# Sink values from small transfers, a new order at the start, and a hold on five weight pieces

## The chip, the cores and the metric

The kernel runs on one core of a Trainium2 chip. The metric is device time in microseconds (us), the median of several executions. The engines named below are TensorE (PE, matrix products into PSUM), VectorE (DVE), ScalarE (ACT), GpSimd (POOL, which here prepares masks and issues the loads that change the type from float32 to bfloat16) and SyncE (SP, which issues plain transfers and transposing transfers).

## The reference

An attention over 4 batches, 8 heads, 768 positions and 64 features per head, in which each position sees the 128 positions up to itself and the first 4 positions (the sinks), followed by a multiplicative feed-forward part on the 3072 rows of 512 features:

```
keep = (key position < 4) | ((0 <= query - key) & (query - key < 128))
a    = softmax(q k^T / 8, over the kept keys);   x = a v   (rows: batch and position, columns: head and feature)
out  = ((x w1) * (x w2)) w3 w_out
```

Shapes: w1 and w2 are 512 x 1024, w3 is 1024 x 1024, w_out is 1024 x 512. Inputs and output are float32; the kernel multiplies in bfloat16.

## The kernel before

**Folding.** w3 w_out is computed first, on the chip, into w3o (1024 x 512), so that each row of the output needs one product with w3o instead of two. For each of eight blocks of 128 rows of w3 the block is transposed by PE (fold_w3, `tp`, 2 x 4 matmuls with the identity), copied from PSUM by DVE (L413), and multiplied with the eight blocks of w_out (fold_mm, `ph` or `pw`, 4 x 2 matmuls, two blocks sharing one `ph`). The result is copied to w3o by ACT (L445, L442). For three blocks of w3 POOL's loads change the type. The other five, and all of w_out in four pairs of blocks, come as nine uncast pieces of 512 KB, issued by SP at the very start (load_raw, L162) into buffers that are free until later: ab of both batches, and kN, qN and kqT of batch 1. ACT or DVE casts each (L418). In this text they are pieces 1 to 9 in the order of issue. `hold` makes POOL wait for the fifth piece ahead of its first load (a one-column copy to `spent`, L201).

**Attention.** Per batch, q, k and v are loaded in blocks of 128 positions (load_qkv, L108, three transfers each, in POOL's order), transposed to kqT (by PE and DVE in batches 0 and 1, by SP's transposing transfers in batches 2 and 3), and scored per pair of heads (`sc`); ACT takes the exponential, DVE multiplies with a mask (`am`), PE multiplies with v (`av`), DVE normalizes. The sinks have a product of their own: `sp` are the scores of the four sink keys of all heads, `es` their exponentials, and `vs` a matrix with the sink rows of v spread so that row 32 (h // 2) + 4 (h % 2) + s holds head h, sink s. `vs` is made by sink_values: a selection matmul of PE (`vp`, L232, with the selection matrix `pick`) and a multiply of DVE with the pattern `ones_s` (L234).

**Feed-forward.** Gates (`pg`, L391): four matmuls with w1, ACT copies, four with w2, DVE multiplies into ab. Then `po` (L452) with w3o, ACT copies, SP stores.

**What sets the order.** Every step is a task with a list of engines and estimated times. A planner (plan) goes through them three times in estimated time, choosing PE's next step by when it can start and by priority, and only the last pass emits instructions. So the tables `raws` (order of the nine pieces and the engine that casts each), `order` (POOL's loads), `nudge` (changes of single priorities), PACE (distance of score steps per batch), the arrival model landings() and the times per task decide in what order PE, ACT, DVE and SP stand. Each engine then goes through its own instructions strictly in that order and waits on semaphores. Where the planner sees PE wait over 0.5 us near the start, keep_busy emits filler matmuls (`pz`, L466) whose result is not used. PSUM has four buffers for most products and two for scores.

Of the kernel before, what the change touches and what calls it, by code (L numbers as in the profile page):

```python
# [21 lines left out]
def kernel(  # L22
# [13 lines left out]
    nc = tc.nc  # L36
# [8 lines left out]
    P = 128  # L45
# [8 lines left out]
    XPOSE = (2, 3)  # L54
# [15 lines left out]
    pick = const.tile([P, P], BF16, name="pick")  # L70
# [56 lines left out]
    def load(what, *i):  # L127
# [9 lines left out]
        else:  # L137
# [12 lines left out]
    nudge = {}  # L150
# [17 lines left out]
    casts = [load_raw(n, *x) for n, x in enumerate(raws)]  # L168
# [5 lines left out]
    nc.vector.memset(pick[:], 0.0)  # L174
    for b in range(B - 1):
        nc.vector.memset(ksbd[b][:], 0.0)

# [16 lines left out]
    pk = pick[:].rearrange("p (r x) -> p r x", x=32)  # L194
    for e in range(2):
        nc.gpsimd.tensor_copy(pk[:, :, 4 * e:4 * e + 4],
                              ident[:, 0:4].rearrange("p (r s) -> p r s", r=1).to_broadcast([P, NP, 4]))
    for b in range(B):
        nc.gpsimd.tensor_copy(vs[b][:, :, D], ones_s[:])
    if hold:  # L200
        nc.gpsimd.tensor_copy(spent[:], casts[hold - 1][1][:, 0:1])  # L201
# [27 lines left out]
    def sink_values(b):  # L229

        vp = ps_mm.tile([P, H, D], FP32, tag="mm", name="vp")
        nc.tensor.matmul(vp[:], pick[:], vN[b][:, 0, :, 0:D], start=True, stop=True)  # L232
        yield
        nc.vector.tensor_mul(vs[b][:, :, 0:D], vp[:],  # L234
                             ones_s[:].rearrange("p (h o) -> p h o", o=1).to_broadcast([P, H, D]))
        yield
# [232 lines left out]
    arrive = {}  # L469

# [10 lines left out]
    def landings(taken, RAW=2.0, POOL=3.0, DGE=1.3, RAMP=(0.6, 0.95, 0.85, 0.9)):  # L481

        queues = {"sp": [(RAW, 1.28, 1.0, [("raw",) + x[:3]]) for x in raws],
# [5 lines left out]
        while any(at[n] < len(q) for n, q in queues.items()):  # L489
# [17 lines left out]
            for n in busy:  # L507
                i = int(now - RAW) if now >= RAW else 0
                share = 1.0 if len(busy) == 1 else 0.5 if small not in "kqv" else 0.79 if n == "sp" else 0.13
                left[n][at[n]] -= 0.02 * share * (RAMP[i] if i < len(RAMP) else 1.0)  # L510
                if left[n][at[n]] <= 0.0:
                    lag, keys = queues[n][at[n]][2:]
                    for key in keys:
                        arrive[key] = now + lag
                    if n == "pool":
                        landed.append(now + lag)
                    at[n] += 1
# [12 lines left out]
    for n, ((what, i0, i1, e), ap) in enumerate(zip(raws, casts)):  # L530
        task(("c", what, i0), n, cast(e == "act", *ap), [(e, 1.04 if e == "act" else 0.69)],
             loads=[("raw", what, i0, i1)])
        made.update({(what, i): ("c", what, i0) for i in range(i0, i1)})

    def need(what, i):
        return ([made[what, i]], []) if (what, i) in made else ([], [(what, i)])

    for i in range(KFF):
        for h in range(2):
            j0, j1 = 4 * h, 4 * h + 4  # L540
            needs = [need("w3", i)]
# [20 lines left out]
    for b in range(B):  # L562
        for t in range(NT):
# [3 lines left out]
            for kb in kbs:  # L567
                if b in XPOSE:
# [8 lines left out]
            if t == 0:  # L577
                task(("sk", b), 0, sink_keys(b), [("dve", 0.2)], [("sc", b, 1, 0)])
                task(("sv", b), 2, sink_values(b), [("pe", 0.22), ("dve", 0.7)],
                     [("av", b - 2, NP - 1, NT - 1), ("av", b, 1, 0)] if b >= 2 else [], [("v", b, 0)], "mm")  # L580
            else:
# [3 lines left out]
                elif t == 1:  # L585
                    more = [(n, b, kb) for n in (("tdk", "tdq") if b in XPOSE else ("tpk",)) for kb in (4, 5)]
# [23 lines left out]
            for r in range(NP):  # L610
                after = list(qk)
                if b >= 2 and t == 0:
                    after.append(("g", b - 2, len(CHUNKS[b - 2]) - 1, KFF - 1, 1))
# [21 lines left out]
    for b in range(B):  # L635
        for c, (t0, t1) in enumerate(CHUNKS[b]):
            last_t = (t1 - 1) // 256
            us = 0.65 * (t1 - t0) / 384
            for dt in range(KFF):
                n = dt * P // 256  # L640
                pr = 1000 + 200 * b + 10 * c + dt
                war = [("p", b - 2, NB - 1)] if b >= 2 else []
                task(("g", b, c, dt, 0), pr + 0.5, gate(b, c, dt, 0), [("pe", us), ("act", 0.2 + us / 2)],
                     ([("xd", b, last_t, 0), ("xd", b, last_t, 1)] if (b, last_t) in X_XPOSE else
                      [("xt", b, NP - 2, last_t)]) + war, [("w1", n), ("w2", n)], "mm",
# [4 lines left out]
            for m in range(t0 // P, t1 // P):  # L650
                cuts = (0, DM // 2, 3 * DM // 4, DM) if (b, m) == (B - 1, NB - 1) else (0, DM)
                for n0, n1 in zip(cuts, cuts[1:]):
# [4 lines left out]
                         [("g", b, c, KFF - 1, 1), *[folded(i) for i in range(KFF)]], ring="mm")  # L657
# [6 lines left out]
    PACE = [0.0, 2.6, 5.5, 4.5]  # L664
# [4 lines left out]
    def plan(emit):  # L669
# [16 lines left out]
        def pe_pick():  # L686
            best = None
            for k in tasks.values():
# [16 lines left out]
                if k["paced"]:  # L705
                    busy = max(0.0, free["act"] - free["pe"]) + sum(q[2] for q in queue["act"])
                    est = max(est, free["pe"] + busy - BACKLOG, last_sc + (PACE[k["name"][1]]))
# [125 lines left out]
```

## Time and profile before

| what | value |
|---|---|
| median of 3 runs | 198.28 us (197.68 to 198.59) |
| profiled execution | 197.16 us, of which its span (first to last instruction) 195.5 us |
| granted TensorE clock | 1.00 of full speed |
| busy share of the span | PE 96%, DVE 59%, ACT 53%, POOL 39% |
| PE, matmuls | 187.9 us in 1818 records |

Busy time of PE holds the filler as well. "DMA share" in a view of stretches is the mean busy share of the 16 DMA engines, counted per queue, so that it can exceed 1. A row of the timeline gives start, duration, engine, line, operation, what it writes and reads, and in brackets the engine's idle time just before with what ended it. A row of the chain gives start, duration and what the work that ended last was doing then; the duration there is the time until the next step, so it shows PE's pace, while a single matmul's duration in the timeline holds its pipeline too.

### The profile page before, as it was taken

The numbers are of one execution on the slowest core, as the hardware profiler recorded it, in microseconds if no ns is written. First come the engines' busy times: TensorE is split into PE (matmuls) and PEld (weight loads), VectorE is DVE, ScalarE is ACT, GpSimd is POOL, SyncE is SP. The second block draws the span as 40 slices with busy tenths as digits, with TensorE's granted clock in tenths as the row PEclk, the third lists the DMA queues.
The fourth block names the chain that finished last, engine by engine and source line by source line (L and its number), as shares of the span: only waits on it lengthen the run. The fifth ranks groups of instructions, "written<-read, shape, count | busy, mean of one in ns | idle before, by whom it ended". The sixth has DMA issues, their size and how long they took to land.

```text
span 195.5 us, 4615 instructions
## 1 busy us (share of the span) xinstructions
PE 187.9 (96%) x1818; PEld 123.4 (63%) x1831; DVE 115.2 (59%) x276; ACT 104.2 (53%) x176; POOL 75.5 (39%) x104
## 2 busy tenths in 40 slices
PE   7689999999999999999999999999999999999993
PEld 2245566888776687888886555566666666644443
DVE  4456696755989888678575426678788344410000
ACT  4242569635776876565565646657583333333232
POOL 5189967689999953433553330000000000000000
PEclk9999999999999999999999999999999999999999
DMA  6999999999999999999999999999220200014334
GB/s 225 401 362 156 179 162 197 194 159 154 155 150 183 180 176 114 156 159 145 137 155 155 149 159 191 239 208 155 49 54 2 57 0 0 0 57 161 143 134 152
DMA packets 107429, 29.14 MB, mean 149 GB/s; under 512 B 98448, under 2 KB 102928, under 8 KB 107408
## 3 DMA queue, kind: packets, MB, share of 16 engines
q0 software_dynamic: 79520, 12.33, 90.3%
q1 hardware_dynamic: 27744, 16.46, 40.6%
q8 instruction: 14, 0.23, 0.5%
q10 hardware_dynamic: 144, 0.07, 0.1%
q14 instruction: 7, 0.06, 0.1%
HBM read 29.36 MB, written 6.29 MB: 182 GB/s over the span
## 4 chain that ended last, share of the span: by engine, by line
PE 86%; DMA 7%; POOL 3%; DVE 1%; issue 1%; SPq 1%; ACT 0%; DVEq 0%
PE pg L391 39%; PE po L452 21%; PE av L351 6%; PE sc L261 5%; DMA ab<-in_moe_w_dram 4%; PE pw L438 4%; DMA qN<-in_q_dram 3%; PE ph L438 3%; PE tp L211 2%; PE tp L408 2%; PE av L314 1%; PE sc L282 1%; POOL vN L108 1%; POOL qN L108 1%; POOL kN L108 1%; PE sp L243 1%
## 5 line engine op out<-in xcount | busy, mean ns | idle before, releaser
L391 PE MATMUL pg<-xT,w_sb 128*128 128x256 bf16 (+1 forms) x640 | 91.5, 294 | 0.0
L391 PEld LDWEIGHTS <-w_sb 128*128 128x128 bf16 x640 | 59.7, 98 | 20.2 <-issue 0.9
L398 ACT COPY a_sb<-pg 128x256 f32<-128x256 f32 (+1 forms) x80 | 33.2, 415 | 40.2 <-PE pg L391 22.7
L395 DVE TENSOR_TENSOR ab<-a_sb,pg 128x256 bf16<-128x256 f32 (+1 forms) x80 | 37.8, 472 | 25.5 <-PE pg L391 21.2
L452 PE MATMUL po<-w3o,ab 128*128 128x512 bf16 (+2 forms) x200 | 42.7, 362 | 0.4
L266 ACT ACTIVATE ex<-sc 128x1024 bf16<-128x1024 f32 (+1 forms) x40 | 38.0, 962 | 5.7 <-PE sc L261 3.9
L452 PEld LDWEIGHTS <-ab 128*128 128x128 bf16 x208 | 19.1, 98 | 20.6 <-issue 0.6
L270 DVE TENSOR_TENSOR am<-ex,maskt 128x1024 bf16<-128x1024 bf16 (+1 forms) x40 | 25.4, 646 | 5.3 <-ACT ex L266 5.2
L108 POOL DMA_DIRECT2D kN<-in_k_dram x24 | 22.4, 931 | 12.8 <-DMA qN<-in_q_dram 10.1
L456 ACT COPY w_sb<-po 128x512 f32<-128x512 f32 (+2 forms) x25 | 14.1, 564 | 24.2 <-PE po L452 24.2
L108 POOL DMA_DIRECT2D qN<-in_q_dram x24 | 22.1, 921 | 9.9 <-DMA vN<-in_v_dram 7.4
L108 POOL DMA_DIRECT2D vN<-in_v_dram x24 | 21.9, 912 | 7.2 <-DMA kN<-in_k_dram 5.1
L358 DVE TENSOR_TENSOR xn<-av,rec 128x256 bf16<-128x256 f32 x40 | 17.0, 425 | 1.4
L351 PE MATMUL av<-vN,am 128*128 128x65 bf16 x296 | 16.7, 193 | 0.0
L351 PEld LDWEIGHTS <-am 128*128 128x128 bf16 x296 | 14.4, 97 | 2.1 <-DVE am L270 0.2
L355 DVE RECIPROCAL rec<-av 128x4 f32<-128x4 f32 x40 | 7.2, 179 | 10.3 <-PE av L351 9.9
L456 DVE COPY w_sb<-po 128x128 f32<-128x128 f32 x1 | 0.3, 292 | 19.7 <-ACT w_sb L456 19.7
L261 PE MATMUL sc<-kqT 64*128 64x128 bf16 (+1 forms) x216 | 11.6, 238 | 0.0
L351 PE MATMUL av<-vs,es 128*128 128x130 bf16 x56 | 11.1, 220 | 0.0
L213 DVE COPY kqT<-tp 128x1024 bf16<-128x1024 bf16 x12 | 8.3, 689 | 3.2 <-PE tp L211 3.1
L438 PE MATMUL ph<-wo_sb,w3t 128*128 128x512 bf16 x31 | 8.0, 380 | 2.0 <-ACT wo_sb L418 1.3
L286 ACT ACTIVATE ex<-sc 128x1024 bf16<-128x1024 f32 x7 | 7.0, 1026 | 5.3 <-PE sc L282 5.3
(71 smaller groups left out, 136.0 us busy)
## 6 DMA issues: line engine op xcount, KB each, us to landing
out_dram<-w_sb SPq DMA_DIRECT2D x23, 256.0 KB, 5.0
kN<-in_k_dram POOLq DMA_DIRECT2D x24, 128.0 KB, 8.0
qN<-in_q_dram POOLq DMA_DIRECT2D x24, 128.0 KB, 8.1
vN<-in_v_dram POOLq DMA_DIRECT2D x24, 128.0 KB, 7.9
w_sb<-in_moe_w_dram POOLq DMA_DIRECT2D x9, 256.0 KB, 8.6
ab<-in_moe_w_out_dram SPq DMA_DIRECT2D x3, 512.0 KB, 6.2
ab<-in_moe_w_dram SPq DMA_DIRECT2D x3, 512.0 KB, 7.0
kN<-in_moe_w_out_dram SPq DMA_DIRECT2D x1, 512.0 KB, 9.3
```

The source lines that it names most:

```text
L108: nc.gpsimd.dma_start(out=dst, in_=rows(src, b, kb))
L261: nc.tensor.matmul(sc[:, e, c:c + n], kT[b][hp, r, kb * P:(kb + 1) * P], qT[b][hp, r, qb * P:qb * P + n], start=True, stop=True)
L266: nc.scalar.activation(ex[:, :, c0:], sc[:, :, c0:], ACTF.Exp, scale=scale)
L270: nc.vector.tensor_mul(am[:, :, c0:], ex[:, :, c0:], mk)
L351: nc.tensor.matmul(o, lhs, rhs, start=(n == 0), stop=(n == len(todo) - 1), skip_group_check=True)
L358: nc.vector.tensor_mul(xns[b, t][:, :, r, :, :], av[:, :, :, 0:D], rec[:].to_broadcast([P, 2, 2, D]))
L391: nc.tensor.matmul(pg[:], w_sb[:, kk, dt * P:(dt + 1) * P], xT[b][:, kk, tk], start=(kk == 0), stop=(kk == NP - 1))
L395: nc.vector.tensor_mul(ab[b][:, dt, tk], gate_a.pop((b, c, dt))[:], pg[:])
L398: nc.scalar.copy(a_sb[:], pg[:])
L438: nc.tensor.matmul(po, w3T[i][:, j, :], wo_sb[:, j, :], start=(j == 0), stop=(j == KFF - 1))
L452: nc.tensor.matmul(po[:], ab[b][:, kk, m * P:(m + 1) * P], w3o[:, kk, n0:n1], start=(kk == 0), stop=(kk == KFF - 1))
L456: (nc.vector.tensor_copy if n0 == DM // 2 else nc.scalar.copy)(o_sb, po[:])
```

## The change

- **Sink values.** The matrix `pick` and the selection matmuls go. A new buffer `vc` (128 x 4 x 64, float32, cleared by DVE) gets the sink rows of all four batches by eight transfers, one per head, each of 4 rows x 4 batches x 64 values (4 KB), issued by SP behind the nine pieces. sink_values is now a single multiply of DVE, `vc` of the batch spread over the heads times `ones_s`, without a wait for v's load and without a PSUM buffer.
- **The nine pieces.** Another order: w_out 2-3, w3 4, w3 0, w_out 0-1, w3 1, w_out 4-5, w_out 6-7, w3 2, w3 3. Two of them ("both") are cast in halves by DVE and ACT.
- **The hold.** Only four pieces are issued at once. DVE then copies one column of piece 2 into the place where piece 5 will lie, so that piece 5's transfer, and with it all that follow on SP, waits until piece 2 has landed.
- **POOL's loads.** The block w3 5 stands ahead of the first k, q, v block.
- **The planner.** Four nudges, PACE per batch and chunk, another arrival model, dependences of gates, scores and output products on all steps they read; transposing transfers are now listed per batch and chunk (the same ones as before). These move instructions; they add none.

```diff
-    XPOSE = (2, 3)
+    XPOSE = ((2, 0), (2, 1), (2, 2), (3, 0), (3, 1), (3, 2))
...
-    pick = const.tile([P, P], BF16, name="pick")
+    vc = const.tile([P, B, D], FP32, name="vc")
...
-    raws = [("wo", 0, 2, "act"), ("w3", 0, 1, "dve"), ("wo", 2, 4, "act"), ("w3", 1, 2, "dve"),
-            ("wo", 4, 6, "act"), ("w3", 2, 3, "dve"), ("wo", 6, 8, "act"), ("w3", 3, 4, "dve"), ("w3", 4, 5, "dve")]
+    raws = [("wo", 2, 4, "act"), ("w3", 4, 5, "act"), ("w3", 0, 1, "both"), ("wo", 0, 2, "dve"),
+            ("w3", 1, 2, "dve"), ("wo", 4, 6, "dve"), ("wo", 6, 8, "dve"), ("w3", 2, 3, "both"),
+            ("w3", 3, 4, "act")]
...
-    order = [("qkv", 0, 0, 1), ("w3", 5, 6), ("qkv", 0, 1, 2), ("w3", 6, 8), ("qkv", 0, 2, 3),
+    order = [("w3", 5, 6), ("qkv", 0, 0, 1), ("qkv", 0, 1, 2), ("w3", 6, 8), ("qkv", 0, 2, 3),
...
-    nudge = {}
+    nudge = {("g", 0, 2, 6, 0): -300, ("g", 1, 2, 4, 0): -1200, ("g", 0, 1, 3, 1): 60, ("fm", 6, 3): 1500}
...
-    casts = [load_raw(n, *x) for n, x in enumerate(raws)]
+    ahead = 4
+    casts = [load_raw(n, *x) for n, x in enumerate(raws[:ahead])]
...
-    nc.vector.memset(pick[:], 0.0)
+    nc.vector.memset(vc[:], 0.0)
     for b in range(B - 1):
         nc.vector.memset(ksbd[b][:], 0.0)
+    home, at = homes[ahead]
+    nc.vector.tensor_copy(home[:, at:at + 1], casts[1][1][:, 0:1])
+    casts += [load_raw(n, *x) for n, x in enumerate(raws) if n >= ahead]
...
-    pk = pick[:].rearrange("p (r x) -> p r x", x=32)
-    for e in range(2):
-        nc.gpsimd.tensor_copy(pk[:, :, 4 * e:4 * e + 4],
-                              ident[:, 0:4].rearrange("p (r s) -> p r s", r=1).to_broadcast([P, NP, 4]))
...
+    for h in range(H):
+        r0 = 32 * (h // 2) + 4 * (h % 2)
+        nc.sync.dma_start(out=vc[r0:r0 + 4, :, :], in_=v[:, h, 0:4, :].rearrange("b s d -> s b d"))
...
-        vp = ps_mm.tile([P, H, D], FP32, tag="mm", name="vp")
-        nc.tensor.matmul(vp[:], pick[:], vN[b][:, 0, :, 0:D], start=True, stop=True)
-        yield
-        nc.vector.tensor_mul(vs[b][:, :, 0:D], vp[:],
+        nc.vector.tensor_mul(vs[b][:, :, 0:D], vc[:, b:b + 1, :].to_broadcast([P, H, D]),
...
-    def landings(taken, RAW=2.0, POOL=3.0, DGE=1.3, RAMP=(0.6, 0.95, 0.85, 0.9)):
+    def landings(taken, RAW=2.0, POOL=3.0, DGE=1.3, RAMP=(0.75, 1.0)):
...
+        cuts = ((0, 1024, e),) if e in ("act", "dve") else ((0, 512, "dve"), (512, 1024, "act"))
+        for c0, c1, eng in cuts:
+            name = ("c", what, i0, c0)
...
-    PACE = [0.0, 2.6, 5.5, 4.5]
+    PACE = [[0, 1.3, 0], [0, 0, 0], [6.2, 0, 0], [5.3, 0, 0]]
```

More of the change, by code (lines that the diff above doesn't have):

```diff
@@ L469 @@
     arrive = {}
+    arrive["vc",] = 20.0
     def service(what, *i):
@@ L612 @@
                 if b >= 2 and t == 0:
-                    after.append(("g", b - 2, len(CHUNKS[b - 2]) - 1, KFF - 1, 1))
+                    after += [("g", b - 2, len(CHUNKS[b - 2]) - 1, dt, 1) for dt in range(KFF)]
                 lead = r % 2 == 0
@@ L656 @@
                           ("act", 0.1) if n0 > DM // 2 else ("sp", SP_US)],
-                         [("g", b, c, KFF - 1, 1), *[folded(i) for i in range(KFF)]], ring="mm")
+                         [("g", b, c, dt, 1) for dt in range(KFF)] + [folded(i) for i in range(KFF)], ring="mm")
     HOP = 0.2
```

37 lines of the change are left out of this document (20 added, 17 removed).

## The prediction

> **What bounds the kernel now.** The page's shares by engine (in the table above) name TensorE (PE), so I read PE alone in stretches: up to its first real matmul, up to the first transposes of attention inputs, and up to its last matmul. Columns: the stretch, its length, PE busy (matmul records), granted clock, DMA share, GB/s.
>
> ```profile
> 0.00:6.19 6.19, 4.86 (x14) 1.00 0.69 254
> 6.19:18.25 12.06, 9.68 (x71) 1.00 1.32 316
> 18.25:192.43 174.18, 173.37 (x1739) 1.00 1.35 134
> ```
>
> From 18.25 us on PE idles 174.18 - 173.37 = 0.81 us, at full clock. So the middle is bound by PE's own work: an edit there gains what PE no longer executes plus part of those 0.81 us. The last 195.5 - 192.43 = 3.07 us are the final copy and store, which the change leaves alone. The rest is the start: PE's first 6.19 us are only filler matmuls (pz, whose result nobody reads). What the start is worth is read from the chain of waits (start, us, what), which gives PE's pace, and from the timeline, whose casts show when each of the nine uncast 512 KB weight pieces is there: pieces 1, 3 and 5 on ACT, pieces 2, 4, 6 and 9 on DVE (7 and 8 come between 6 and 9 in the same step).
>
> ```profile
> 15.58 2.16 PE ph L438 x10
> 17.74 0.67 PE tp L408 x12
> 18.41 0.45 PE tp L211 x8
> ...
> 19.29 0.22 PE vp L232
> ...
> 20.37 0.33 PE sc L282 x8
> ```
> ```profile
> 4.18 1.04 ACT L418 CAST wo_sb<-ab 128x1024 bf16<-128x1024 f32 x1 [2.10 <-DMA ab<-in_moe_w_out_dram]
> 7.93 1.04 ACT L418 CAST wo_sb<-ab 128x1024 bf16<-128x1024 f32 x1 [2.70 <-DMA ab<-in_moe_w_out_dram]
> 10.49 1.04 ACT L418 CAST wo_sb<-ab 128x1024 bf16<-128x1024 f32 x1 [1.51 <-DMA ab<-in_moe_w_out_dram]
> ```
> ```profile
> 5.42 0.71 DVE L418 CAST w_sb<-ab 128x1024 bf16<-128x1024 f32 x1 [1.82 <-DMA ab<-in_moe_w_dram]
> ...
> 9.21 0.69 DVE L418 CAST w_sb<-ab 128x1024 bf16<-128x1024 f32 x1 [1.83 <-DMA ab<-in_moe_w_dram]
> ...
> 11.75 0.69 DVE L418 CAST w_sb<-ab 128x1024 bf16<-128x1024 f32 x1 [0.60 <-DMA ab<-in_moe_w_dram]
> ...
> 15.96 1.04 DVE L418 CAST w_sb<-kqT 128x1024 bf16<-128x1024 f32 x1
> ```
>
> A product (ph, pw) costs 2.16 / 10 = 0.216 us and a weight transpose (tp) 0.67 / 12 = 0.056 us. Up to 18.25 us the program has done 40 transposes and 28 products, 40 x 0.056 + 28 x 0.216 = 8.29 us of useful work. So 18.25 - 8.29 = 9.96 us are lost at the start, and that is what the change can win or lose there.
>
> The casts stand 1.24 us apart at first (5.42 - 4.18), then 2.51 (7.93), then 1.28, 1.28 and 1.26 (9.21, 10.49, 11.75). Piece 3 is the odd one. The bytes do not show this step: two half microseconds, early and late (last column GB/s), and SP's issues of pieces 7 and 8:
>
> ```profile
> 2.50:3.00 0.50, 0.50 (x2) 0.15 (x1) 0.47 (x3) 0.00 (x0) 0.44 (x1) 1.00 1.03 393
> 13.00:13.50 0.50, 0.22 (x4) 0.10 (x2) 0.46 (x2) 0.48 (x1) 0.50 (x1) 1.00 1.09 426
> ```
> ```profile
> 3.67 0.45 SPq L162 DMA_DIRECT2D kN<-in_moe_w_out_dram  x1
> 4.16 0.99 SPq L162 DMA_DIRECT2D qN<-in_moe_w_dram  x1
> ```
>
> At some 400 GB/s a piece of 0.524 MB takes 1.3 us, so bytes run evenly while piece 3 and all after it arrive 2.51 - 1.28 = about 1.2 us later than pieces 1 and 2 would lead one to expect. I write 1.1 us for it below, to leave something to rounding.
>
> **The change, part by part.**
>
> *Start: other order of pieces, and a hold.* ACT's casts at the start, before and then now (ab_103, ab_104, kN_88, qN_84, kqT_96 are buffers of later stages in which the pieces lie):
>
> ```order
> L169 ACT_TABLE_LOAD
> L418 CAST wo_sb<-ab_103 128x1024 x2
> L418 CAST wo_sb<-ab_104 128x1024
> L418 CAST wo_sb<-kN_88 128x1024
> L445 CAST w3o<-ph 128x1024
> ```
> ```order
> L171 ACT_TABLE_LOAD
> L419 CAST wo_sb<-ab_103 128x1024
> L419 CAST w_sb<-ab_103 128x1024
> L419 CAST w_sb<-ab_103 128x512
> L419 CAST w_sb<-qN_84 128x512
> L446 CAST w3o<-ph 128x1024
> L419 CAST w_sb<-kqT_96 128x1024
> ```
>
> ACT now casts piece 2 and, behind the copy of the first folded pair (w3o), piece 9. DVE at the same place, before and now:
>
> ```order
> L418 CAST w_sb<-ab_103 128x1024
> L413 COPY w3t<-tp_197 128x512
> L413 COPY w3t<-tp_202 128x512
> L418 CAST w_sb<-ab_104 128x1024
> L413 COPY w3t<-tp_218 128x512
> ```
> ```order
> L180 CAST ab_104<-ab_103 128x1
> L414 COPY kN_88<-tp_204 128x512
> L414 COPY kN_88<-tp_209 128x512
> L419 CAST w_sb<-ab_103 128x512
> L419 CAST wo_sb<-ab_104 128x1024
> L414 COPY w3t<-tp_221 128x512
> L414 COPY w3t<-tp_226 128x512
> L419 CAST w_sb<-ab_104 128x1024
> L419 CAST wo_sb<-ab_104 128x1024
> L414 COPY w3t<-tp_251 128x512
> ```
>
> The first row now is the hold (one column, waits for piece 2; SP's fifth piece waits for it). Behind it the casts of pieces 4 and 6 stand ahead of transposed blocks that PE needs. The fifth piece is issued at about 5.42 + 0.2 = 5.6, where the seventh was before it by 3.67. Four pieces keep the DMA busy until about 7.5 (2.1 MB at 400 GB/s take 5.2 us, and the bytes run before 2.5), so hardly a gap arises: with an empty queue it is there no later than 5.6 + 4.18 = 9.8 (as if piece 1 had been issued at 0), below the 10.49 of before. Whether pieces 3 to 9 arrive at the old times or 1.1 us earlier no row shows. For the old times speaks that pieces 1 and 2 were quick although the seventh was issued before the first had landed (3.67 and 4.18); for the earlier ones that the eighth issue took 0.99 us instead of 0.45, just ahead of the late piece. I take the old times, the rows that exist, and keep the other end for the range. One more price, ACT's copy of a folded pair:
>
> ```profile
> 16.05 1.01 ACT L445 CAST w3o<-ph 128x1024 bf16<-128x1024 f32 x1 [1.99 <-PE ph L438]
> ```
>
> With those landings: piece 2 is cast 5.42 to 6.46, 8 transposes end at 6.9. Piece 3 (7.93), cast in halves by both engines, gives 8 transposes until 8.8. The first product needs piece 4: 9.21 + 0.69 + hop = 9.95; 8 products to 11.7, 8 transposes of piece 5 to 12.15. Then the products need piece 6, 11.75 + 0.69 = 12.45: 0.35 idle, 12 products to 15.1. Until 16.85 the 8 transposes of piece 8 and 6 products run. PE then needs piece 9 cast by ACT, which first copies the pair finished at 15.8: 15.8 + 1.01 + 1.04 = 17.85, so 1.0 us idle. The 8 transposes and 6 products behind end at 19.65, where the attention transposes stand. By then 40 transposes and 32 products are done, 9.15 us; lost are 19.65 - 9.15 = 10.5 us, against 9.96: **+0.55 us**. With pieces 3 to 9 earlier by 1.1 it is 0.55 - 1.1 = -0.55.
>
> *Sink values.* Four selection matmuls leave PE, 0.22 us each: **-0.88 us**. The one of batch 1 had also waited for its load:
>
> ```profile
> 48.61 0.60 PE L391 MATMUL pg<-xT,w_sb 128*128 128x256 bf16 x4
> 49.30 0.39 PE L232 MATMUL vp<-vN,pick 128*128 128x512 bf16 x1
> ```
>
> A gate of 4 matmuls takes 0.44 (the chain's last row below), so PE was free at 49.05 and waited 0.25 us: **-0.25 us**, since the attention products that need the same load stand later. DVE's multiply reads SBUF instead of PSUM; I leave it at its old price. The larger memset (vc for pick) is covered by DVE's 1.82 us of waiting ahead of piece 2. Two copies leave POOL, hidden by its wait for piece 5 (the bracket of its first row below). Eight loads of 4 KB go on SP, which until the first store has nothing else to issue. Here is also the stretch of the chain that shows gates and loads:
>
> ```profile
> 47.09 6.50 DMA qN<-in_q_dram
> 53.59 0.05 issue
> 53.64 0.40 PE tp L211 x4
> 54.04 0.44 PE pg L391 x4
> ```
> ```profile
> L234 DVE TENSOR_TENSOR vs<-vp,ones_s x4: 686/690/694, 19.6 to 126.7; 128x512 bf16<-128x512 f32 x4
> ```
> ```profile
> 10.51 0.19 POOL L201 COPY spent<-ab 128x1 f32<-128x1 f32 x1 [4.93 <-DMA ab<-in_moe_w_out_dram]
> ...
> 13.78 0.57 POOL L125 DMA_DIRECT2D w_sb<-in_moe_w_dram  x1
> ```
>
> *PE's order later, pacing, transposes as a list per chunk.* The same matmuls in other places; the list names the same chunks. With 0.81 us of idle in 174 it can win at most that. A loss has no row; from the waits that the kernel shows for a misplaced step (0.25 us a piece) I bound it at +1.5 (six of them) and take 0. POOL now loads a w3 block ahead of the first k, q and v (0.57 us of issue), and the first transposes stand 1.4 us later, which covers it.
>
> *Sum.* +0.55 - 0.88 - 0.25 = -0.58. The profiled execution took 197.16 us (span 195.5 and 1.66 around it), so 196.6; the median of the runs shown, 198.28, stands 1.12 above it: **197.7 us**.
>
> **The rivals.**
>
> *Earlier pieces.* If holding back five pieces takes the step off pieces 3 to 9: -0.55 - 0.88 - 0.25 = -1.7 us. Some is given back later, where PE stands at the loads' heels: in the chain piece above the transposes at 53.64 waited for a load of 6.50 us. POOL starts its loads when piece 5 is there, so they also come earlier; I give back 0.3. Time 196.9. If only pieces 3 and 4 gain, PE waits for pieces 5 and 6 as above, and nothing is won: that is the forecast again, and so is a hold without any effect.
>
> *The sink rows come late (slower).* The eight loads and the multiply that reads them, first on SP, then DVE's rows there before and now (the multiply had its input from PE's vp):
>
> ```order
> L163 DMA ab_104<-in_moe_w_out_dram 128x1024
> L163 DMA kN_88<-in_moe_w_out_dram 128x1024
> L163 DMA qN_84<-in_moe_w_dram 128x1024
> L163 DMA kqT_96<-in_moe_w_dram 128x1024
> L203 DMA vc<-in_v_dram 4x4x64 x8
> L460 DMA out_dram<-w_sb 128x512 x3
> ```
> ```order
> L213 COPY kqT_95<-tp 128x8x128
> L234 TENSOR_TENSOR vs_111<-vp,ones_s 128x8x64
> L413 COPY qN_84<-tp_333 128x512
> L290 TENSOR_TENSOR am<-ex,maskt 128x1024
> L213 COPY kqT_95<-tp 128x8x128
> ```
> ```order
> L414 COPY qN_84<-tp_309 128x512
> L217 COPY kqT_95<-tp 128x8x128
> L235 TENSOR_TENSOR vs_111<-vc,ones_s 128x8x64
> L414 COPY w3t<-tp_330 128x512
> L414 COPY w3t<-tp_350 128x512
> ```
>
> The loads stand behind all nine pieces, and the last one waits, by its semaphore, for the ninth piece. The multiply now waits for all eight on DVE, with two copies behind it that PE needs. The last load is issued at about 15.96 + 0.45 = 16.4. What a small transfer takes beside POOL's loads no row shows; the nearest are stores from SP, at the kernel's end with POOL idle, then beside POOL's loads at 57 to 60 and at 64 to 70 us, and the transposes:
>
> ```profile
> out_dram<-w_sb SPq DMA_DIRECT2D x1, 64.0 KB, 1.7
> out_dram<-w_sb SPq DMA_DIRECT2D x1, 256.0 KB, 5.0
> out_dram<-w_sb SPq DMA_DIRECT2D x1, 256.0 KB, 7.7
> kqT<-kN SPq DMA_TRANSPOSE x12, 8.2
> ```
>
> So it lands between 18.1 and 24.6. Past 20.1 (19.65 and 0.45 for the transposes) PE has 2.5 us of work that does not need those copies: 8 weight transposes (0.45), 6 products (1.3), a block of scores (0.33) and the next attention transposes (0.45). That is until 22.6; the multiply and a copy (0.42 in the row below) come first, 0.69 + 0.42.
>
> ```profile
> 15.62 0.42 DVE L413 COPY w3t<-tp 128x512 bf16<-128x512 bf16 x1 [0.49 <-PE tp L408]
> ```
> The case decides from 22.6 - 1.1 = 21.5 on. 4 KB has few packets, so I expect 1.7 to 5.0 us, 18.1 to 21.4: just in time. At 7.7 us it would cost 24.1 - 21.5 = 2.6 us, time 197.7 + 2.6 = 200.3.
>
> The Trainium skill, DMA: Bandwidth & Descriptors, section Queues, rings and completion order, says that a transfer's semaphore write lands only after every earlier write of that DMA engine, across its queues. By it a 4 KB load would be held up by POOL's loads on the same engines, nearer to 7.7 than to 1.7 us, and the time would be 200.3; no row of a small load beside POOL's traffic is there to say. The same page's Rules for kernel authors would have small transfers joined into one, at about 2 us fixed each; by its figure the last lands at 18.4 (an estimate from that page), and nothing would wait.
>
> **How the numbers follow.** Forecast 0.35 (its own range 197.3 to 198.7, from 0.4 us of the 0.81 won to 1 us of misplaced waits); earlier pieces 0.36, 196.2 to 197.3; late sink rows 0.17, 199.0 to 200.9; misplaced steps in the middle beyond 1 us 0.12, 198.7 to 199.8. The range from 196.2 to 200.2 leaves out the worst of the late rows and a little below the earlier pieces. A measurement of this kernel tells about 0.5%, 1 us. Faster by over that (below 197.3): 0.36 and a tail of the forecast, 0.40. Slower (above 199.3): 0.17 and half of the misplaced steps, 0.23. Within: the rest, 0.37.
>
> **What would show it.** Landing: the third cast starts at 7.9 (forecast) or 6.8 (earlier pieces); the fifth piece's issue at 5.6. Start: the first attention transposes at about 19.7, with an idle of 1 us on PE ahead of the transposes of piece 9; a start at 18.6 is the first rival. Sink rows: DVE waiting for vc ahead of its first multiply, and PE for the copies behind it, is the second rival. PE's idle time from there to the last matmul should stay under 1 us; if it is 2 or more, the order in the middle is what I had wrong. Wrong is all of it if the step after piece 2 is not there for a reason that I did not see.

## The result, and the profile after

The changed kernel takes 196.43 us (median of 8, 195.78 to 197.83) against 198.28 (197.68 to 198.65) for the kernel before, measured beside it: ratio 0.992, 95% interval 0.9893 to 0.9948. Measured once more on another occasion it took 196.81 against 198.38 (ratio 0.9959, 0.9922 to 0.9996). Here and below the ratios are taken from fast executions alone, while the medians and ranges hold all executions. By the medians the gain is 1.6 to 1.9 us; by the middles of the ratios it is 0.8 to 1.6.

The profiled execution of the changed kernel was one of its slower ones: 197.57 us, span 195.9. Its lines answer to those of before. PE in stretches (up to its first real matmul, to the first transposes of attention inputs, to its last matmul; the columns are those of the prediction):

```profile
0.00:6.96 6.96, 5.58 (x13) 1.00 0.74 272
6.96:18.80 11.84, 10.74 (x78) 1.00 1.38 304
18.80:192.82 174.02, 172.07 (x1741) 1.00 1.34 134
```

The casts of pieces 1, 2, 3, 4, 5, 6 and 9, with the hold (the copy of one column, L180) and SP's fifth issue:

```profile
4.60 1.04 ACT L419 CAST wo_sb<-ab 128x1024 bf16<-128x1024 f32 x1 [2.52 <-DMA ab<-in_moe_w_out_dram]
5.86 1.04 ACT L419 CAST w_sb<-ab 128x1024 bf16<-128x1024 f32 x1 [0.21 <-DMA ab<-in_moe_w_dram]
5.86 0.16 DVE L180 CAST ab<-ab 128x1 bf16<-128x1 f32 x1 [2.07 <-DMA ab<-in_moe_w_dram]
6.05 0.33 SPq L163 DMA_DIRECT2D ab<-in_moe_w_dram  x1
7.15 0.62 ACT L419 CAST w_sb<-ab 128x512 bf16<-128x512 f32 x1 [0.24 <-DMA ab<-in_moe_w_dram]
8.41 0.69 DVE L419 CAST wo_sb<-ab 128x1024 bf16<-128x1024 f32 x1
10.71 0.69 DVE L419 CAST w_sb<-ab 128x1024 bf16<-128x1024 f32 x1 [0.93 <-DMA ab<-in_moe_w_dram]
11.89 0.71 DVE L419 CAST wo_sb<-ab 128x1024 bf16<-128x1024 f32 x1 [0.49 <-DMA ab<-in_moe_w_out_dram]
17.00 1.05 ACT L419 CAST w_sb<-kqT 128x1024 bf16<-128x1024 f32 x1
```

Piece 3 now comes 1.29 us behind piece 2 (before: 2.51), but piece 5's cast comes 2.30 behind piece 4's: the step moved two pieces back. PE's rows around the end of the start, and its two new waits (the second one as a group: waiter, releaser, us, times, longest):

```profile
12.65 1.02 PE L439 MATMUL ph<-wo_sb,w3t 128*128 128x512 bf16 x4 [0.57 <-DVE wo_sb L419]
...
17.05 0.40 PE L409 MATMUL tp<-ident,w_sb 128*128 128x128 bf16 x4
...
18.80 0.39 PE L215 MATMUL tp<-ident,kN 128*128 128x128 bf16 x4
...
25.96 0.40 PE L409 MATMUL tp<-ident,w_sb 128*128 128x128 bf16 x4 [1.06 <-DMA w_sb<-in_moe_w_dram]
```
```profile
PE sc L262 <- DMA kqT<-qN: 0.9, 1, 0.9
```

A second profile of the same kernel (execution 196.15 us, span 194.4) starts the attention later, at 19.44, but has neither of the two waits; behind 19.44 PE idles 0.08 us:

```profile
7.03:19.44 12.41, 10.57 (x78) 1.00 1.41 292
19.44:191.39 171.95, 171.87 (x1741) 1.00 1.35 135
```

By the sum of the prediction the two traces divide like this, against the trace of before (195.5). The start is the time of the first attention transposes less 9.15 us of work, against 9.96; the middle is the last row's length against 174.18 - 0.86 (four products now done at the start) - 0.88 (selection matmuls) = 172.44; the end (span less last matmul) was 3.07.

| | first profile | second profile |
|---|---|---|
| start | 18.80 - 9.15 - 9.96 = -0.31 | 19.44 - 9.15 - 9.96 = +0.33 |
| selection matmuls | -0.88 | -0.88 |
| middle | 174.02 - 172.44 = +1.58 | 171.95 - 172.44 = -0.49 |
| end | +0.01 | -0.06 |
| sum | +0.40: 195.9 | -1.10: 194.4 |

One kernel's traces thus differ by 1.5 us from one execution to the next, as much as the change is worth. What a part is worth is therefore read below from medians; the traces say by which wait.

### The profile page after: what moved, and what is told of

Same layout as the page of the kernel before. It is cut to its first block, busy times and chain, and to the rows that moved or that the text cites. A ratio compares the mean times of both kernels' runs of the same rounds, so it can differ in the third digit from the quotient of the medians.

```text
span 195.9 us, 4626 instructions
## 1 busy us (share of the span) xinstructions
PE 188.4 (96%) x1830; PEld 123.6 (63%) x1830; DVE 114.6 (58%) x278; ACT 104.0 (53%) x177; POOL 75.5 (39%) x102
## 4 chain that ended last, share of the span: by engine, by line
PE 80%; DMA 13%; POOL 4%; SPq 1%; issue 0%; DVE 0%; ACT 0%; POOLq 0%
PE pg L392 39%; PE po L453 21%; PE av L352 6%; PE sc L262 5%; DMA ab<-in_moe_w_dram 5%; DMA w_sb<-in_moe_w_dram 4%; DMA kqT<-qN 4%; PE tp L215 2%; PE pw L439 2%; SPq L379 1%; POOL qN L108 1%; PE av L315 1%; POOL vN L108 1%; PE sp L244 1%; PE sc L283 1%; POOL kN L108 1%
## 5 line engine op out<-in xcount | busy, mean ns | idle before, releaser
L271 DVE TENSOR_TENSOR am<-ex,maskt 128x1024 bf16<-128x1024 bf16 (+1 forms) x40 | 25.4, 647 | 10.4 <-ACT ex L267 10.3
L108 POOL DMA_DIRECT2D kN<-in_k_dram x24 | 21.9, 914 | 11.8 <-DMA qN<-in_q_dram 9.2
L457 DVE COPY w_sb<-po 128x128 f32<-128x128 f32 x1 | 0.3, 293 | 19.7 <-ACT w_sb L457 19.7
L262 PEld LDWEIGHTS <-kqT 64*128 64x128 bf16 x216 | 7.0, 94 | 5.3 <-issue 4.7
```

What stands on the lines that cost most here:

```text
L108: nc.gpsimd.dma_start(out=dst, in_=rows(src, b, kb))
L262: nc.tensor.matmul(sc[:, e, c:c + n], kT[b][hp, r, kb * P:(kb + 1) * P], qT[b][hp, r, qb * P:qb * P + n], start=True, stop=True)
L271: nc.vector.tensor_mul(am[:, :, c0:], ex[:, :, c0:], mk)
L457: (nc.vector.tensor_copy if n0 == DM // 2 else nc.scalar.copy)(o_sb, po[:])
```

## Experiments

**The hold, taken out of the changed kernel and put into the one before.** Neither edit moves any other instruction of PE, ACT or SP.

```diff
-    casts = [load_raw(n, *x) for n, x in enumerate(raws[:ahead])]
+    casts = [load_raw(n, *x) for n, x in enumerate(raws)]
...
-    home, at = homes[ahead]
-    nc.vector.tensor_copy(home[:, at:at + 1], casts[1][1][:, 0:1])
-    casts += [load_raw(n, *x) for n, x in enumerate(raws) if n >= ahead]
```

> The changed kernel with all nine pieces issued at once and without DVE's copy of one column; every instruction else stands in the same place. Changed kernel: 196.43 us. Theory H (the hold takes the step of 1.2 us off the third piece and puts it behind the fourth): the third cast goes back to about 7.9 to 8.4 us, the fifth and all later pieces land as before or up to 0.3 us sooner; PE's first product comes about 1 us later, and the first attention transposes, 18.80 us in the changed kernel, stand at 19.3 to 19.8; time about 197.0. Theory N (the hold moves nothing that PE waits for, since in both kernels the pieces from the fifth on land late): transposes at 18.8, time 196.4. Theory O (the step belongs to the order of the pieces or to their rows in memory and not to how many are issued): the third cast stays at 7.2.

Measured: 196.91 us (195.79 to 199.08), ratio to before 0.9916 (0.9885 to 0.9947): the changed kernel's own ratio. The other way round (the three lines added to the kernel before):

> The kernel before plus the hold alone: the same instructions on PE and ACT, one copy of one column more on DVE. Kernel before: 198.28 us, third cast at 7.93, fourth 9.21, fifth 10.49, first attention transposes at 18.25. Theory H: third and fourth cast about 1.2 us earlier (6.7 and 8.0), the fifth at 10.5 to 10.7 as before. PE's products of the start then run ahead only until they need the fifth piece, so little is won: transposes at 17.9 to 18.25, time 197.9 to 198.3. Theory E (the step goes for all pieces): fifth cast at 9.4, transposes at 17.1, time 197.2. Theory N: all casts as before, 198.3.

Measured: 198.73 us (198.11 to 200.82) against 198.19, ratio 1.005 (1.0015 to 1.0084): slower by 0.5 us by the medians, by 1.0 (0.3 to 1.7) by the ratio. Casts of pieces 2, 3 and 5 without the hold in the new order (first fence), and of pieces 2 to 5 with it in the old order (second):

```profile
5.61 1.04 ACT L416 CAST w_sb<-ab 128x1024 bf16<-128x1024 f32 x1 [0.47 <-DMA ab<-in_moe_w_dram]
...
7.68 0.62 ACT L416 CAST w_sb<-ab 128x512 bf16<-128x512 f32 x1 [1.03 <-DMA ab<-in_moe_w_dram]
...
10.24 0.69 DVE L416 CAST w_sb<-ab 128x1024 bf16<-128x1024 f32 x1
```
```profile
5.41 0.71 DVE L422 CAST w_sb<-ab 128x1024 bf16<-128x1024 f32 x1
...
8.25 1.04 ACT L422 CAST wo_sb<-ab 128x1024 bf16<-128x1024 f32 x1 [3.08 <-DMA ab<-in_moe_w_out_dram]
9.54 0.69 DVE L422 CAST w_sb<-ab 128x1024 bf16<-128x1024 f32 x1 [2.18 <-DMA ab<-in_moe_w_dram]
11.26 1.04 ACT L422 CAST wo_sb<-ab 128x1024 bf16<-128x1024 f32 x1 [1.96 <-DMA ab<-in_moe_w_out_dram]
```

Without the hold the new order has the step at piece 3 (2.07 us) and gets piece 5 at 10.24, earlier than with it. With the hold the old order still has the step at piece 3 (2.84) and pays 1.72 between pieces 4 and 5, so that piece 5 comes 0.8 us later than the 10.49 of before. So the hold does not take the step away: in the old order it is there with four pieces in the queue as with nine, and theories H and E fall. In the new order piece 3 does come sooner with the hold, at 7.15 against 7.68, but a third of the smaller step (1.29 against 2.07) is that piece 2 comes later, at 5.86 against 5.61. Theory H falls in the new order too, since there the attention transposes stood at 18.36 without the hold, earlier than in either profile with it. The hold is worth nothing that these runs can tell in the new order, and costs 0.5 to 1.0 us in the old one.

**The sink values alone, in the old order.** The planner is told of the old steps, so PE, ACT and DVE keep their order; of PE's work only the selection matmuls go, and POOL's two copies that made `pick` go with them:

```diff
-        vp = ps_mm.tile([P, H, D], FP32, tag="mm", name="vp")
-        nc.tensor.matmul(vp[:], pick[:], vN[b][:, 0, :, 0:D], start=True, stop=True)
         yield
-        nc.vector.tensor_mul(vs[b][:, :, 0:D], vp[:],
+        nc.vector.tensor_mul(vs[b][:, :, 0:D], vc[:, b:b + 1, :].to_broadcast([P, H, D]),
...
+    for h in range(H):
+        r0 = 32 * (h // 2) + 4 * (h % 2)
+        nc.sync.dma_start(out=vc[r0:r0 + 4, :, :], in_=v[:, h, 0:4, :].rearrange("b s d -> s b d"))
```

> The kernel before plus the sink values alone: no selection matmuls, eight loads of 4 KB on SP behind the nine pieces, one multiply of DVE that waits for them; all other instructions of PE, ACT and DVE stand in the order of before. My sum: four matmuls of 0.22 us and 0.25 us of waiting for v's load gone, 198.28 - 0.88 - 0.25 = 197.15. If the 0.25 us only move to the next product that needs the load or PE waits elsewhere for the same loads: 197.4 to 198.0. If the eight loads (which here are issued at about 5 to 7 us, ahead of nothing on SP) hold up a piece or land after 21.5 us: 198.3 or more.

Measured: 197.74 us against 198.19, ratio 0.9976 (0.9949 to 1.0004). The medians are 0.45 us apart, under half of the 1.13 us of my sum, and the interval reaches both no gain and 1 us. Which term is too large this run does not show.

**Hold and sink values together, in the old order** (both edits above).

> The kernel before plus hold and sink values, in the order of before. What lies between this kernel and the changed one (196.43 us) is the new order alone: pieces, who casts them, POOL's loads, the planner's places. If the parts add up, it takes the time of before plus what the two single edits give. If the order is worth nothing, as I had it for the middle: 196.4. If the order wins at the start (the changed kernel loses 9.65 us there, the one before 9.96) and pays it back in the middle (PE idles 1.95 us there, before 0.81): 196.4 too, but with first attention transposes at 17.9 to 18.3 and under 0.9 us of idle behind them. If the order is what makes the hold pay: 197.2 or more.

Measured: 198.43 us, ratio 1.0012 (0.9988 to 1.0036): no gain at all. By the medians the two single edits add up to +0.54 - 0.45 = +0.09, near the +0.24 here. Between this kernel and the changed one lie only the new order of pieces, casts, loads and steps, and 1.8 to 2.1 us by the medians (+0.24 here against -1.85 and -1.57), 1.1 to 1.8 by the ratios (1.0012 against 0.992 and 0.9959). Its chain of waits, which in the trace of before runs over one late load behind the start, meets five loads that POOL or SP issued:

```profile
17.43 8.13 DMA w_sb<-in_moe_w_dram
...
27.73 8.23 DMA w_sb<-in_moe_w_dram
...
36.24 9.98 DMA kN<-in_k_dram
...
48.25 6.54 DMA qN<-in_q_dram
...
73.05 9.37 DMA kqT<-qN
```

This is one trace: the chain of the hold alone meets no load behind the start and that of the sink values alone one, as against two and one in the two profiles of the changed kernel.

And the sink rows come late here: DVE's first multiply waits for vc, the transposed block copied behind it is late, and PE stands (DVE's row, then PE's):

```profile
21.27 0.69 DVE L235 TENSOR_TENSOR vs<-vc,ones_s 128x512 bf16<-128x512 f32 x1 [1.63 <-DMA vc<-in_v_dram]
```
```profile
22.36 0.61 PE L439 MATMUL pw<-wo_sb,qN 128*128 128x512 bf16 x2 [0.66 <-DVE qN L414]
```

Where the order gains can be read from this trace, which is close to its median (198.34 us) and at full clock. PE's last stretch in it, from the first attention transposes to the last matmul:

```profile
18.21:193.55 175.34, 173.89 (x1747) 1.00 1.35 134
```

The new order has done four products (0.86 us) more ahead of the attention, so that this start answers to 18.21 + 0.86 = 19.07 and this stretch to 175.34 - 0.86 = 174.48. PE has the changed kernel's order in five profiles: the two above, the one without the hold, and two below (without five fillers, and with POOL's loads begun earlier in the same order). In these the attention starts at 18.36 to 19.63, mean 19.03, and the stretch takes 171.95 to 174.02, mean 172.87. So by these traces the order gains nothing at the start and 1.6 us behind it, of which 0.6 are idle time of PE (1.45 against a mean of 0.86) and 1.0 are longer busy time. The base is thin, a single trace of the old order. And the first trace of before, in an execution 1.12 us faster than its median, has the 172.44 us worked out above, no more than the new order.

**What a matmul is worth in the new order.** One filler matmul ahead of each of the four multiplies, all else in place:

```diff
     def sink_values(b):
 
+        keep_busy(1)
         nc.vector.tensor_mul(vs[b][:, :, 0:D], vc[:, b:b + 1, :].to_broadcast([P, H, D]),
```

> The changed kernel plus four matmuls of PE whose result is not used (128 x 512, as long as the removed selection matmuls, 0.22 us each), one ahead of each of DVE's four multiplies for the sink values; all other instructions stand in the same order. Changed kernel 196.43. It measures what a matmul more or less is worth. If PE's own work bounds the middle, as I had it: 196.43 + 0.88 = 197.3. If PE has slack there because it meets loads that come at their own time, as the kernel with hold and sink values in the old order shows (its PE waits 0.3 to 0.7 us in several places between 22 and 54 us): 196.4 to 196.9.

Measured: 197.19 us, ratio 0.9965 (0.9933 to 0.9998). That is 0.76 us above the changed kernel's first median and 0.38 above its second; by the ratios it is 0.9 and 0.1. In the new order four matmuls are thus worth 0.4 to 0.8 us by the medians, and the intervals do not exclude nothing at all; that they count more there than in the old order (0.45) these runs don't show.

**Which part of the order.** The old table of pieces in the changed kernel, and then the old planner's tables in it; in both the planner orders the rest anew.

```diff
-    raws = [("wo", 2, 4, "act"), ("w3", 4, 5, "act"), ("w3", 0, 1, "both"), ("wo", 0, 2, "dve"),
+    raws = [("wo", 0, 2, "act"), ("w3", 0, 1, "dve"), ("wo", 2, 4, "act"), ("w3", 1, 2, "dve"),
...
```

> The changed kernel with the old table of the nine pieces (their order and the engine that casts each); hold, sink values, POOL's loads and the planner's tables stay new, and the planner orders the rest anew. If the gain of 2.0 us that the new order brings over hold and sink values alone (198.43 against 196.43) is made at the start, by the pieces and the fillers that stand between them: 197.9 to 198.5. If it is made in the middle, by steps that stand later than their loads: 196.4 to 196.9. The first attention transposes would stand at 18.2 in the old order of pieces (with 8.29 us of work ahead of them), 18.8 in the new (9.15).

```diff
-    nudge = {("g", 0, 2, 6, 0): -300, ("g", 1, 2, 4, 0): -1200, ("g", 0, 1, 3, 1): 60, ("fm", 6, 3): 1500}
+    nudge = {}
...
-    def landings(taken, RAW=2.0, POOL=3.0, DGE=1.3, RAMP=(0.75, 1.0)):
+    def landings(taken, RAW=2.0, POOL=3.0, DGE=1.3, RAMP=(0.6, 0.95, 0.85, 0.9)):
...
-                        arrive[key] = now + lag + min(2.5, max(0.0, 0.25 * (now - 36.0)))
+                        arrive[key] = now + lag
...
-    PACE = [[0, 1.3, 0], [0, 0, 0], [6.2, 0, 0], [5.3, 0, 0]]
+    PACE = [[0] * 3, [2.6] * 3, [5.5] * 3, [4.5] * 3]
```

> The changed kernel with the old nudges (none), the old pacing and the old arrival model; pieces, casts, POOL's loads, hold and sink values stay new, and the planner orders the rest anew. The opposite of the run with the old pieces. Gain made in the middle: PE waits for loads again, 2 us or more of idle between the first attention transposes and the last matmul, time 197.5 to 198.5. Gain made at the start: 196.4 to 197.0.

Measured: 202.27 us (ratio 1.0225, 1.0172 to 1.0279) and 201.83 us (1.0185, 1.0118 to 1.0252). Both are 5 to 6 us slower than the changed kernel and slower than the one before, which neither theory allowed. The waits of PE that are new (old pieces first, then old planner's tables):

```profile
PE pg L391 <- DMA xT<-xn: 2.2, 1, 2.2
PE sc L261 <- DMA kqT<-qN: 2.1, 1, 2.1
```
```profile
PE sc L262 <- DMA kqT<-qN: 1.9, 2, 1.8
...
PE tp L215 <- DMA qN<-in_q_dram: 0.8, 2, 0.5
```

The large ones are single waits of about 2 us for transposing transfers behind 90 us, two in the first kernel and one in the second; the wait for qN in the last row is for POOL's loads, at 43 to 46 us. So the parts of the order can't be priced by putting one of them back: every edit gives another order of some thousand steps, and whether a score or a gate then meets its transfer decides over microseconds.

**POOL's chain of loads, begun earlier.** POOL waits for piece 4 instead of piece 5, first with the planner told, then with it not told (same order on all engines as the changed kernel).

```diff
-    hold = 5
+    hold = 4
```

> The changed kernel, but POOL's first load waits for the fourth piece (cast at 8.41 us in the changed kernel) and not for the fifth (10.73); the planner knows of it. If PE's waits in the middle come from POOL's chain of loads, which begins at that wait (18.80 + 1.95 us of idle in the profile of the changed kernel, of which 1.06 us for the w3 load that POOL issued at 17.99): the loads come up to 2 us earlier, the pieces 6 to 9 later by what the loads take from them, time 195.7 to 196.2. If the bytes are the limit and not their start: 196.4. If the pieces suffer more than the loads gain: 197 or more.

```diff
-        nc.gpsimd.tensor_copy(spent[:], casts[hold - 1][1][:, 0:1])
+        nc.gpsimd.tensor_copy(spent[:], casts[hold - 2][1][:, 0:1])
```

> The changed kernel with POOL's first load behind the fourth piece instead of the fifth, but with every instruction of all engines in the order of the changed kernel (the planner is not told). The run with the planner told took 201.19, of which 3.4 us are one wait for a transposing transfer at 137 us, a place that the new order of steps made; so it said nothing on the earlier loads. If PE's waits for k, q, v and w3 at 21 to 26 us come from when POOL's chain of loads begins: the chain begins at about 8.9 instead of 10.7, the waits (0.7 to 1.1 us in three profiles of kernels with this order) are gone, the time is 195.4 to 196.0. If the pieces that are left pay for it (sixth and later casts later than 11.9, 13.2, 14.5): 196.4 or more.

Measured: 201.19 us (ratio 1.0158, 1.011 to 1.0207) and 197.06 us (0.9943, 0.9912 to 0.9975); the changed kernel stood at 196.81 beside the latter. The first is again a replanned order with one large wait; the second shows what the earlier loads do. Rows of the first, then of the second (the casts of pieces 6 and 8, and DVE's multiply):

```profile
PE pg L392 <- DMA xT<-xn: 3.4, 1, 3.4
```
```profile
12.27 0.71 DVE L419 CAST wo_sb<-ab 128x1024 bf16<-128x1024 f32 x1 [1.16 <-DMA ab<-in_moe_w_out_dram]
...
15.65 0.43 DVE L419 CAST w_sb<-qN 128x512 bf16<-128x512 f32 x1 [1.35 <-DMA qN<-in_moe_w_dram]
...
22.35 0.70 DVE L235 TENSOR_TENSOR vs<-vc,ones_s 128x512 bf16<-128x512 f32 x1 [1.38 <-DMA vc<-in_v_dram]
```

POOL's first load goes out 1.9 us earlier (the gate at 8.80 against 10.73). PE no longer waits for a load at 21 to 26 us, but pieces 6 and 8 are cast 0.4 and 1.15 us later than in the first profile of the changed kernel (11.89 and 14.50) and 0.1 and 0.9 later than in the second (12.16 and 14.74), the attention starts at 19.63, and vc lands late enough to hold up DVE. So the pieces and the sink rows pay for what the loads gain, and the time is the changed kernel's within what these runs can tell.

**The fillers.** The five filler matmuls at 7.4 and 9.0 us taken out of the changed kernel:

```diff
-                    if emit:
+                    if emit and start < 7.3:
                         keep_busy(int((gap - 0.25) / (0.22 if start > 9.0 else 0.43)))
```

> The changed kernel without the five filler matmuls at 7.4 and 9.0 us (those of the first 6.9 us stay). Nothing waits for them. In the two profiles in which PE idled 2.46 and 2.67 us between 5.8 and 10.2 us, the eight products behind took 3.4 to 3.6 us instead of 1.9 at half the granted clock; with 1.95 and 2.2 us of idle they did not. Without the fillers PE idles about 0.53 + 5 x 0.22 to 5 x 0.43 = 1.6 to 2.7 us there. If idle time of this size takes the clock down: products at 10 to 13 us at half speed, 1.0 to 1.7 us later, part of it given back at the loads, time 196.6 to 197.5. If the clock does not depend on it: 196.4.

Measured: 196.96 us (ratio 0.9942, 0.9908 to 0.9975) against 196.81 for the changed kernel beside it: no difference. PE idled 1.36 us ahead of the row at 7.07 and 0.96 ahead of the one at 8.66, and its clock stayed at 1.00. These 2.32 us are less than the 2.42 and more after which the clock fell elsewhere, so the run does not settle whether the clock depends on idle time.

**Both kernels once more.**

> The kernel before once more, unchanged, for a second profile. Its profiled execution took 197.16 us, 1.12 us less than its median. If the kernel before waits in most executions for loads that were just in time in that one, PE idles in more than the four places of the start, with 0.5 us or more of waiting for loads behind 18 us. If its executions differ at the start: the third cast stands later than 7.93.

> The changed kernel once more, unchanged, for a second profile and beside the run below on the same chip. Its profiled execution had 1.06 us of waiting at 25.96 for a w3 load and 0.9 us at 97 us for a transposing transfer, and took 197.57, 1.14 us above its median. If both waits are chance: they are gone or smaller, the span is about 194.8. If they belong to the kernel: they are there again. Median 196.4.

Measured: 199.04 us for the single execution of before, 196.81 us for the changed kernel (its second profile stands above). The second profile of before differs at the start, though not by its casts (the third at 7.95): PE's clock, in tenths by slices of 4.9 us, falls in the third one, and eight products take 3.44 us where they took 1.90.

```profile
PEclk9969999999999999999999999999999999999999
```
```profile
9.04 0.59 PE L438 MATMUL ph<-wo_sb,w3t 128*128 128x512 bf16 x2 [1.33 <-ACT wo_sb L418]
...
10.90 3.44 PE L438 MATMUL ph<-wo_sb,w3t 128*128 128x512 bf16 x8
```

In the middle it waits twice for transposing transfers (0.36 us at 82, 0.55 at 124), which its first profile did not.

The traces of the hold alone and of the sink values alone, in the old order too, have the same stretch at half the clock, and their attention starts at 19.90 and 19.71, as here at 19.59, against 18.25 and 18.21 in the two traces of the old order without it. It is a rival for the gain, since no trace of the changed kernel's order has it. But one such stretch lowers the mean clock of an execution to 0.99, and 0.989 to 0.992 stands in 5 of 78 executions of the kernel before beside these runs, in 6 of 36 of its three kernels with one or both edits, and in none of 65 of the kernels with the changed kernel's order. At about 1.4 us each, 5 of 78 come to 0.1 us in the mean: too few to make a gain of 1.6 to 1.9 in the median.

## Why the prediction came out as it did

The direction was right. 196.43 and 196.81 lie inside 196.2 to 200.2, but 0.9 to 1.3 us below the 197.7 forecast and outside the forecast's own 197.3 to 198.7. The time is the one that I gave to the earlier pieces (196.9), and that mechanism is not what made it: piece 5 is cast at 10.71 and 10.43, against 10.49 before. That the time fell into the range was luck as far as the reasons go.

- **Start, +0.55: failed in one row.** I had PE wait 1.0 us for piece 9, ahead of the weight transposes at about 17 us. The transposes at 17.05 are not piece 9's: ACT's cast of piece 9 runs from 17.00 to 18.05 beside them, and they read the w3 block that POOL's first load brings. The w3 blocks are folded in the order 4, 0, 1, 2, 5, then the first attention inputs, then 3; piece 9 (block 3) is needed only behind 19 us. Without that 1.0 the step gives -0.45; the two profiles show -0.31 and +0.33, the other three with this order of PE -0.75, -0.20 and +0.52. The rest of the walk held: first product 9.95 forecast, 9.65 and 9.72 measured; idle time ahead of piece 6's products 0.35 forecast, 0.57 and 1.31 measured.
- **Hold, 0: about right in the changed kernel.** I had it as without effect, or as moving pieces 3 and 4 alone. In the changed kernel it did the latter (7.15 and 8.41, against 7.68 and 8.97 without it). In the old order it delayed pieces 3 and 5 and cost 0.5 to 1.0 us, a loss that I had not allowed for.
- **Sink values, -0.88 - 0.25: right in kind, too large in the old order.** 0.45 us there by the medians. In the new order four matmuls put back cost 0.4 to 0.8; the new order without the sink values was not run.
- **Order in the middle, 0: mis-sized, and the main error.** I read 0.81 us of idle time as the most that an order could win. Hold and sink values with the old order gain nothing (198.43), and the order brings 1 to 2 us from there; my own price for all of it was +0.55. The bound looked at idle time in one execution of the old order, which was 1.12 us faster than the median, and I then added these 1.12 us to the changed kernel, as if no edit could touch what makes a typical execution slower. Without them the sum gives 196.6, close to what was measured, though its parts were not the right ones. The trace of hold and sink values in the old order, close to its median, is 1.6 us longer behind the start than the mean of the new order, and equal ahead of it. So one trace puts the gain in the middle, where I had 0. That the steps of the new order stand better to their transfers fits the idle part of it (0.6 us), but it is argued and not shown, and which of the tables makes the gain stays open.
- **Its other end, +1.5 from six waits of 0.25: too small.** Three replanned kernels were 4 to 6 us slower than the changed kernel, with single waits of 1.8 to 3.4 us for transposing transfers. The case was rightly on the list, at a price of half or less.
- **Late sink rows: the place was right.** I had the last of the eight loads landing between 18.1 and 21.4, just in time, and a loss from 21.5 on. In the first profile DVE's multiply at 20.05 waited for nothing, in the second it waited 0.19 us until 20.97. In the old order with the hold vc came at about 21.2 and did cost PE 0.66 us, 0.3 us before the point that I gave; with POOL's loads begun earlier it came at 22.35. The changed kernel was thus 0.5 us away from this rival in the second profile and at least 1.4 in the first.
- **What I said would show it.** The third cast came at 7.15 (between 6.8 and 7.9), the fifth issue at 6.05 (5.6 said), the attention transposes at 18.80 and 19.44 (19.7 said, without the wait of 1 us). Idle time behind them was 1.95 and 0.08 us: by my bound the middle order would have been wrong in one execution and right in the other, so the idle time of one execution was a poor sign to go by.

No run is faster than the changed kernel by more than these runs can tell.

## What to carry to other kernels

Do not bound what an order of steps can win by the idle time of one execution, least of all a fast one: 0.81 us of idle time stood in an execution 1.12 us faster than the median, and the new order was worth 1 to 2 us. Two edits that gained nothing together in the old order stand in a kernel 1.6 to 1.9 us faster; that the new order needs them for it was not shown, and without the hold it was as fast. Before a wait is put on a row, find out which load that row reads; a name such as "w_sb" stood for eight blocks with two kinds of sources. And where single executions of one kernel differ by as much as the change, take sizes from medians and only mechanisms from traces.

## What was not expected of the hardware

**The step in landings has several faces.** In the first trace of before, bytes ran at 361 to 426 GB/s from 4.5 to 8.5 us while piece 3 came 1.2 us late. In other kernels the rate itself fell for half a microsecond or more; DMA share and GB/s are the last columns, the new order without hold, the old order with the hold (at both places of its steps) and the old order with the sink loads alone:

```profile
5.00:5.50 0.50, 0.50 (x2) 0.15 (x1) 0.00 (x0) 0.14 (x1) 0.41 (x4) 1.00 0.56 188
```
```profile
5.00:5.50 0.50, 0.50 (x4) 0.20 (x2) 0.17 (x2) 0.17 (x1) 0.50 (x5) 1.00 0.90 262
...
7.50:8.00 0.50, 0.19 (x1) 0.00 (x0) 0.00 (x0) 0.00 (x0) 0.00 (x0) 1.00 0.60 238
```
```profile
5.00:5.50 0.50, 0.50 (x4) 0.20 (x2) 0.00 (x0) 0.26 (x1) 0.41 (x4) 1.00 0.32 123
```

What makes either step stays open; the old order with the hold shows that it needs no more than four pieces in the queue.

**A load of 4 KB took 4.7 us beside POOL's loads.** With POOL's loads begun earlier, the chain has the last of the eight from its issue to its landing:

```profile
17.54 4.73 DMA vc<-in_v_dram
```

POOL's own w3 load, issued at 17.99 in the first profile after, took 7.9 us. The Trainium skill, DMA: Bandwidth & Descriptors, section Queues, rings and completion order, would have the small load's semaphore wait for every earlier write of its DMA engine. The same page gives about 2 us as the fixed cost of a transfer, a fit for loads that GpSimd issues. The 4.7 us here, for a load from SP, are more than that and less than POOL's loads took; whether earlier writes make up the difference no run here shows.

**Half the clock after idle time, but not always.** In three profiles with the old pieces PE idled 2.42, 2.49 and 2.67 us between 5.8 and 10.3 us, and the products behind ran at half speed for some 3.5 us; with 1.95 and 2.21 us in that stretch, and with 2.32 us in the kernel without fillers, they did not. Single long waits are no clearer. One of 3.40 us at 134 us, in the profiled execution of the replanned kernel with the earlier gate, left the clock at 1.00. One of 2.10 us, in the kernel with the old pieces, did not: from 138.2 to 141.4 the granted clock was 0.50, and eight gate matmuls took 2.74 us, where eight of the same shape took 1.47 at 143.99.

```profile
137.73 0.61 PE L261 MATMUL sc<-kqT 64*128 64x256 bf16 x10 [2.10 <-DMA kqT<-qN]
...
138.61 2.74 PE L391 MATMUL pg<-xT,w_sb 128*128 128x384 bf16 x8
```

So a wait for a transfer can cost more than its own length. What decides was not tested further.
